# Linear attention and a swish MLP on one core: batch 0 by halves of its heads, and the order of two sets of sums in block 6

## The chip, the cores and the metric

The kernel runs on one core of one Trainium2 chip. The metric is device time in microseconds (us). Engines are named as in the profile: PE (TensorE matmul), PEld (its weight loads), DVE (VectorE), ACT (ScalarE), POOL (GpSimd) and SP (SyncE, which only issues transfers here).

## The reference

Linear attention over 8 batches of 8 heads, 576 tokens and 64 features a head, then an MLP from 512 to 2048 and back over all 4608 tokens. Inputs and output are float32; the kernel works in bf16 with float32 sums.

```python
def phi(x):
    return np.where(x > 0, x, np.exp(x) - 1.0) + 1.0
q_p, k_p = (phi(q), phi(k))
kv = np.einsum('bhsd,bhse->bhde', k_p, v)
z = np.sum(k_p, axis=2)
num = np.einsum('bhsd,bhde->bhse', q_p, kv)
den = np.einsum('bhsd,bhd->bhs', q_p, z)[..., None] + 1e-06
x = (num / den).transpose(0, 2, 1, 3).reshape(B * S, H * D)
h = x @ w_in
g = h * (1.0 / (1.0 + np.exp(-beta * h)))
y = g @ w_out
```

## The kernel before

The order of the instructions on every engine is written out by hand. Work goes in blocks: block b computes h, g and y of batch b, and the attention of the batches after it (phi, kv, numerators) is put between the products as side work. Of a batch's 576 tokens, 512 go through its block as four tiles of 128; the ninth part of all batches (64 tokens each, `xT_tail`) makes a ninth block of 512 at the end. h is made in 16 tiles of 128 features ("f tiles"); each goes through silu on ACT into `g_sb`.

**Start.** Batch 0 has nothing to hide behind, so its attention is PE's critical work. SP loads q and k of batch 0 in two halves each (heads 0 to 3 and 4 to 7, called `pr` 0 and 1). POOL issues, in this order, v of batch 0 in two halves, w_in in four parts, two parts of w_out, q and k of batch 1 (`load`, L99); the last two wait for v's halves, whose counters they take over. phi is exp on ACT (`phi_exp`), max on DVE (`phi_relu`) and min on DVE (`phi_min`). PE transposes phi of q (`q_half`, `q_last` for the last 64 tokens) into banks from which `q_copy` and `q_copy_last` fill `qT`.

Then, for all heads at once: `z_sums` (L519) sums phi of k over the tokens, half by half; `kv_first` (L530) makes k'v; `zbd` (L557) and `kv_mask` (L539) put both into block form on DVE; `denom_mm` (L571) makes the denominators of a token tile for all heads, `denom` (L578) adds 1e-6 and inverts. `numer_first` (L591) makes a token tile's numerators for all heads and multiplies on DVE into `xs_sb` (L595, 512 columns); `x_first` transposes the tile's four 128x128 parts on PE (L385) and copies them into `xT` (L242 on ACT). `h_first(t)` adds the products of the four k parts for token tile t in f tiles 0 to 3, 16 products of 128 columns (L405). The last, half token tile (t = 4) goes to `xT_tail` before `h_first(3)`. After that f tiles 4 to 15 run plain, with four products of 512 columns each, and then Y of batch 0 (L420).

`idle(n)` is n products of 512 columns on constant data, which keep PE at work.

PSUM has two pools of four banks in this stage: `bank` (tag h) and `bank1` (tag f). Tiles take the banks in turn, so a tile waits for the last reader of the tile four before it. `hp0`, the four h banks of f tiles 0 to 3, come from the first pool behind the denominators; f tiles 4 to 7 from the second, behind the numerators and transposes.

**Y of a block** (`y_fast`, L1003) computes the 512x512 output by seven products of 16 instructions in four banks pa, pd, pc and pb, with DVE's sums between:

```python
product(pc, sums(1), wsum(1), True, step=4 if b == 1 else 8)
nc.vector.tensor_add(u2, pc, r1)
nc.vector.tensor_add(u3, pd, u2)
run(side, 3)
```

(L1025 to L1028; `run(side, n)` runs the side work of place n there.) Behind it follow pb, a second product into pd (L1038) and one into pb. Before each block from 3 on, `h_x_sums` (L822) makes four sums of the next block's x, which read `xT` after its transposes (SP, L358). Blocks 7 and 8 use more sums of w_in: `h_w_sums(2)` (L800 to L803) runs in Y of block 6. In Y of block 6 the x sums stand at place 0, ahead of u2 and u3 (L1026, L1027), and the w_in sums at place 4.

Of the kernel before, what the change touches and what calls it, by code (L numbers as in the profile page):

```python
# [16 lines left out]
def kernel(  # L17
# [33 lines left out]
    def bank(name, shape=None, dt=F32):  # L51
        return hps.tile(shape or [P, 512], dt, tag="h", name=name)

    def bank1(name, shape=None, dt=F32):
        return fps.tile(shape or [P, 512], dt, tag="f", name=name)
# [89 lines left out]
    for i in range(2):  # L145
        nc.vector.memset(vaug[i][:, :, :, :, D : D + 2], 1.0)

    warm_ps = bank("warm_ps")

    def idle(n, ps=None):  # L150
# [119 lines left out]
    def q_tile(b):  # L270
        st[b, "qT"] = work.tile([P, 2, NT, 2, P], BF16, tag="qT", name="qT", bufs=1)
# [16 lines left out]
    def rows_of(t):  # L288
        return P if t < NT - 1 else G
# [106 lines left out]
            )  # L396


    def h_mm(x, ff, hp, c0=0, c1=512, kcs=range(KC)):
        for kc in kcs:  # L400
            if x is xT_tail:
                n, xm = G, x[:, kc % 2, :, kc // 2]
            else:
                n, xm = P, x[:, kc % 2, 2 * (c0 // P) + kc // 2 : 2 * (c1 // P) : 2]
            nc.tensor.matmul(  # L405
                hp[:, c0:c1].rearrange("p (t n) -> p t n", n=n),
                w_in_sb[ff // 4][:, kc, (ff % 4) * P : (ff % 4 + 1) * P],
                xm,
                start=(kc == 0), stop=(kc == KC - 1), skip_group_check=True,
            )  # L410

    def silu(b, ff, hp):
# [79 lines left out]
    phi_tile(0, "q")  # L492
    phi_tile(0, "k")
    q_tile(0)
    qtp = [bank1("qtp", [P, 1024], BF16) for _ in range(2)]
    phi_part(0, "q", 0)
    q_half(0, 0, qtp[0])
    idle(4)
    phi_part(0, "q", 1)
    q_half(0, 1, qtp[1])  # L500
    t8 = bank1("qtp8", [P, 2 * P], BF16)
    q_last(0, t8)
    bps = bank("bps", [P, FC])
    nc.tensor.matmul(bps, beta_row, ident16, is_transpose=True, start=True, stop=True)
    idle(4)
    x = xin(0, "k", 0)
    phi_exp(0, "k", 0, x)
    phi_relu(0, "k", 0, x)
    q_copy(nc.vector, 0, 0, qtp[0])
    phi_min(0, "k", 0)  # L510


    zps = [bank("zps") for _ in range(2)]
    zbd = consts.tile([P, 2, 2, 2], BF16)

    def z_sums(pr):
        for j in range(J):
# [3 lines left out]
                    start=(j == 0), stop=(j == J - 1), skip_group_check=True,  # L521
                )

    kvp0 = [[bank1("kvp0") for _ in range(2)] for _ in range(2)]
    kv0 = consts.tile([P, 2, 2, 2 * D], BF16)

    def kv_first(pr):
        for j in range(J):
# [8 lines left out]
    def kv_mask(pr):  # L537
        for hh in range(2):
            nc.vector.tensor_mul(  # L539
                kv0[:, hh, pr].rearrange("p (h d) -> p h d", h=2),  # L540
                kvp0[pr][hh][:, 0:P].rearrange("p (h d) -> p h d", h=2),
                kvmask[:, hh, :, 0:D],
            )

    z_sums(0)
    idle(3)
    phi_part(0, "k", 1)
    q_copy(nc.scalar, 0, 1, qtp[1])
    q_copy_last(nc.scalar, 0, t8)
    nc.scalar.copy(beta_s, bps)  # L550
    table(ACTF.Silu)
    kv_first(0)
    z_sums(1)
    idle(1)
    kv_first(1)
    for hh in range(2):
        nc.vector.tensor_mul(  # L557
            zbd[:, hh], zps[hh][:, 0:2, None].to_broadcast([P, 2, 2]), kvmask[:, :, :, 0]
        )
    kv_mask(0)  # L560

    dps = [bank("dps", [P, NT, 8]) for _ in range(2)]
    den0 = [consts.tile([P, NT, 8], F32, name=f"den0{i}") for i in range(2)]
    rden0 = [consts.tile([P, NT, 8], F32, name=f"rden0{i}") for i in range(2)]

    def denom_mm(t):
        n = rows_of(t)
        for hh in range(2):
            for pr in range(2):
                c = 4 * hh + 2 * pr  # L570
                nc.tensor.matmul(  # L571
                    dps[t > 1][:n, t, c : c + 2], st[0, "qT"][:, pr, t, hh, 0:n],
                    zbd[:, hh, pr, :], start=True, stop=True, skip_group_check=True,
                )

    def denom(r, t0, t1):
        i, ts = t0 > 1, slice(t0, t1)
        nc.vector.tensor_scalar(den0[i][:r, ts], dps[i][:r, ts], 1e-6, None, ALU.add)  # L578
        nc.vector.reciprocal(rden0[i][:r, ts], den0[i][:r, ts])

    for t in range(NT):
        denom_mm(t)
    kv_mask(1)
    denom(P, 0, 2)

    def numer_first(t):
        n = rows_of(t)
        nps = bank1("nps0", [P, 2, 2, P])
        for hh in range(2):
            for pr in range(2):  # L590
                nc.tensor.matmul(  # L591
                    nps[:n, hh, pr], st[0, "qT"][:, pr, t, hh, 0:n], kv0[:, hh, pr, :],
                    start=True, stop=True, skip_group_check=True,
                )
        nc.vector.tensor_mul(  # L595
            xs_tile(0, t),
            nps[:n].rearrange("p a b (c d) -> p a (b c) d", d=D),
            rden0[t > 1][:n, t].rearrange("p (a i) -> p a i", a=2)[:, :, :, None].to_broadcast(
                [n, 2, 4, D]
            ),  # L600
        )

    def x_first(t, eng):
        x_trans(0, t, eng, bank1("xtp0", [P, KC, P], BF16))


    hp0 = []

    def h_first(t):
        if len(hp0) < 4:  # L610
            hp0.extend(bank("h_ps") for _ in range(2))
        for ff in range(4):
            h_mm(xT[0], ff, hp0[ff], t * P, (t + 1) * P)


    hp0.extend(bank("h_ps") for _ in range(2))
    for t in range(3):
        numer_first(t)
        if t == 1:
            denom(P, 2, NT - 1)  # L620
    idle(2, hp0[0])
    denom(G, NT - 1, NT)
    x_first(0, nc.scalar)
    numer_first(3)
    x_first(1, nc.scalar)
    h_first(0)
    numer_first(4)
    x_first(2, nc.scalar)
    h_first(1)
    x_first(3, nc.scalar)  # L630
    nc.vector.tensor_mul(beta_m, beta_s, beta_s)
    nc.vector.tensor_scalar(beta_m, beta_m, TINY * TINY, 2.0 * TINY, ALU.is_lt, ALU.mult)
    nc.vector.tensor_add(beta_c, beta_s, beta_m)
    nc.vector.reciprocal(rbeta, beta_c)
    h_first(2)
    x_first(4, nc.vector)
    h_first(3)
    for ff in range(4):
        silu(0, ff, hp0[ff])
    for ff in range(4, 8):  # L640
        hp = bank1("h_ps")
        h_mm(xT[0], ff, hp)
        silu(0, ff, hp)
    first.close()
    wps = ctx.enter_context(tc.tile_pool(name="wps", bufs=2, space=bass.MemoryType.PSUM))
    load_w_out(2)
# [427 lines left out]
    for b in range(1, B + 1):  # L1074
        n, m = b + 1, b + 2
        sh, sy = {}, {}
        if b == 2 or b == B - 1:
            at(sh, 0, lambda: tail_copy(b))
        if n < B:
            at(sh, 0, lambda: next_loads(n))  # L1080
            if b > 2:
                at(sh, 0, lambda: tail_copy(b))
            at(sh, {1: 9, 2: 3}.get(b, 0), lambda: kv_both(n))
            at(sh, {1: 11, 2: 5}.get(b, 10), lambda: numer_all(n))
        if b == 1:
            at(sh, 4, lambda: w_sum(2))
            at(sh, 9, lambda: w_sum(1))
            at(sy, 0, lambda: w_sum(3))
        if m < B:
            at(sy, 0, lambda: phi_tile(m, "q"), lambda: phi_tile(m, "k"))  # L1090
            if b == 1:

                for pr in range(2):
                    at(sy, 0, lambda pr=pr: phi_exp(m, "q", pr, xin(m, "q", pr)))
                    at(sy, 2, lambda pr=pr: phi_relu(m, "q", pr, xin(m, "q", pr)))
                    at(sy, 3 + pr, lambda pr=pr: phi_min(m, "q", pr))
                for pr in range(2):
                    at(sy, 0, lambda pr=pr: v_copy(nc.scalar, m, pr))
                at(sy, 4, lambda: q_trans_dma(m))
                for pr in range(2):  # L1100
                    at(sy, 5, lambda pr=pr: phi_exp(m, "k", pr, xin(m, "k", pr)))
                    at(sy, 5, lambda pr=pr: phi_relu(m, "k", pr, xin(m, "k", pr)))
                    at(sy, 6, lambda pr=pr: phi_min(m, "k", pr))
                at(sy, 6, lambda: table(ACTF.Silu))
            else:
                at(sy, 0, lambda: phi_part(m, "q", 0))
                at(sy, 1, lambda: phi_part(m, "q", 1))
                at(sy, 1, lambda: q_trans_dma(m))
                at(sy, 4, lambda: phi_part(m, "k", 0))
                at(sy, 4, lambda: phi_part(m, "k", 1), lambda: table(ACTF.Silu))  # L1110
        if b == 2:
            at(sh, 2, lambda: h_w_sums(0))
        if b == B - 2:
            at(sy, 4, lambda: h_w_sums(2))
        if 2 <= b < B:
            at(sy, 6 if b < B - 2 else 0, lambda: h_x_sums(n))
        (h_phase if b < 3 else h_fast)(b, xT[b % 2] if b < B else xT_tail, sh)
        y_fast(b, sy)

# [29 lines left out]
```

## Time and profile before

| what | value |
|---|---|
| three runs | 273.04, 273.45, 274.24 us, median 273.45 |
| profiled execution | 273.47 us, its span 271.7 us |
| mean granted TensorE clock | 0.999 |
| busy share of PE, DVE, ACT, POOL | 97%, 76%, 62%, 16% |
| first h product of batch 0 | 16.77 us |
| Y of batch 0 begins | 32.17 us |
| idle of PE before yd in Y of block 6 | 1.40 us |

Times within the span count from its start. A row of a timeline gives start, duration, engine, line, operation, out<-in, shape and count, and in brackets the engine's idle time before it with what ended it. A row of the chain gives start, duration, engine and tile. The DVE and PE timelines show the end of one instruction after the start of the next, since they are pipelined: 16 products of 256 columns follow each other at 1.75 us and are listed with 1.91.

### The profile page before, as it was taken

The page shows a single profiled execution, that of the slowest core. Times are in us where ns is not written, and L with a number is a line of the kernel's source. Part 1 is how long each engine was busy: PE and PEld are TensorE (multiplying, and loading weights), DVE is VectorE, ACT ScalarE, POOL GpSimd, SP SyncE. Part 2 cuts the span into 40 slices and gives each one's busy share as a digit, 9 for nine tenths or more (in the row PEclk, how much of TensorE's full clock was granted, in tenths as well). Part 3 has the DMA queues.
Part 4 walks back from the last instruction along what each step waited for, and adds up shares of the span by engine and source line. Part 5 has one row for each costly group of instructions (what it writes and reads, how often), then busy time and mean ns, then how long its engine had stood idle before and what let it go on. Part 6 is the DMA issues. An engine that isn't in the chain of part 4 may idle for free.

```text
span 271.7 us, 6793 instructions
## 1 busy us (share of the span) xinstructions
PE 263.0 (97%) x2859; PEld 181.3 (67%) x2865; DVE 207.1 (76%) x404; ACT 167.4 (62%) x236; POOL 43.6 (16%) x65
## 2 busy tenths in 40 slices
PE   7799999999999999999999999999999799999994
PEld 3485455446865587658765876588658666886793
DVE  4871786999996579689968986899686877856862
ACT  5738894977965893599349934994492038405810
POOL 5922005040105003030213003310000100000000
PEclk9999999999999999999999999999999999999999
DMA  7999999997599945995699559945504050023013
GB/s 252 240 207 351 249 320 249 273 183 258 90 247 191 187 78 99 281 210 72 109 257 232 85 91 273 232 86 96 148 7 85 0 154 4 0 51 106 0 41 116
DMA packets 49214, 42.19 MB, mean 155 GB/s; under 512 B 30352, under 2 KB 41248, under 8 KB 49184
## 3 DMA queue, kind: packets, MB, share of 16 engines
q0 software_dynamic: 13296, 22.81, 37.3%
q1 hardware_dynamic: 35568, 18.75, 31.0%
q8 instruction: 22, 0.36, 0.5%
q10 hardware_dynamic: 320, 0.20, 0.2%
q14 instruction: 8, 0.07, 0.1%
HBM read 36.71 MB, written 9.44 MB: 170 GB/s over the span
## 4 chain that ended last, share of the span: by engine, by line
PE 89%; DMA 4%; DVE 2%; SPq 2%; issue 1%; ACT 0%; DVEq 0%; ACTq 0%
PE h_ps L405 36%; PE yd L1003 10%; PE ya L1003 9%; PE yb L1003 8%; PE hc L837 5%; PE yc L1003 5%; PE y_ps L420 4%; PE hz L837 4%; DMA stage<-in_k_dram 3%; PE kvp L226 2%; PE nps L336 2%; DMA xT<-xs_sb 2%; PE yb L975 1%; SPq L358 1%; PE xtp L385 1%
## 5 line engine op out<-in xcount | busy, mean ns | idle before, releaser
L413 ACT ACTIVATE g<-h_ps,beta_c 128x512 bf16<-128x512 f32 x112 | 74.6, 690 | 63.0 <-PE h_ps L405 62.5
L405 PE MATMUL h_ps<-xT,w_in 128*128 128x512 bf16 (+1 forms) x464 | 97.6, 357 | 0.1
L405 PEld LDWEIGHTS <-w_in 128*128 128x128 bf16 x496 | 44.8, 98 | 40.7 <-issue 0.2
L1003 PEld LDWEIGHTS <-stage 128*128 128x128 bf16 x480 | 47.0, 98 | 5.5
L1003 PEld LDWEIGHTS <-g 128*128 128x128 bf16 x384 | 37.5, 98 | 7.6 <-issue 1.6
L1003 PE MATMUL ya<-w_out,g 128*128 128x256 bf16 x256 | 30.6, 273 | 0.0
L351 DVE TENSOR_TENSOR xs_sb<-nps,rden 128x448 bf16<-128x448 f32 (+2 forms) x24 | 18.2, 758 | 0.8
L164 ACT ACTIVATE e<-xk 128x1152 bf16<-128x1152 bf16 (+1 forms) x15 | 16.7, 1159 | 0.2 <-DMA xk<-in_k_dram 0.2
L1003 PE MATMUL yd<-ws,g 128*128 128x256 bf16 x128 | 15.3, 273 | 1.4 <-DVE u L1027 1.4
L164 ACT ACTIVATE e<-xq 128x1152 bf16<-128x1152 bf16 x14 | 15.6, 1160 | 0.0
L157 ACT ACT_TABLE_LOAD x12 | 15.4, 1283 | 0.2
L1003 PE MATMUL yc<-ws,stage 128*128 128x256 bf16 x128 | 15.3, 273 | 0.0
L1003 PE MATMUL yd<-ws,stage 128*128 128x256 bf16 x128 | 15.3, 273 | 0.0
L244 POOL CAST vaug<-vf 128x1152 bf16<-128x1152 f32 x10 | 11.4, 1175 | 22.1 <-DMA vf<-in_v_dram 22.1
L420 PE MATMUL y_ps<-w_out,g 128*128 128x512 bf16 x60 | 14.4, 379 | 0.3 <-issue 0.2
L887 ACT ACTIVATE g<-hc,beta_c 128x512 bf16<-128x512 f32 x16 | 10.1, 683 | 6.4 <-DVE hc L873 6.4
L177 DVE TENSOR_TENSOR phi_q<-e,r 128x1152 bf16<-128x1152 bf16 x16 | 12.1, 757 | 2.3 <-ACT e L164 1.3
L177 DVE TENSOR_TENSOR phi_k<-e,r 128x1152 bf16<-128x1152 bf16 x16 | 12.7, 802 | 1.5 <-DVE r L171 0.5
L746 DVE TENSOR_TENSOR stage<-g 128x1024 bf16<-128x1024 bf16 x16 | 11.0, 686 | 3.2 <-ACT g L413 3.2
L1003 PE MATMUL yb<-w_out,stage 128*128 128x256 bf16 x112 | 13.4, 272 | 0.0
L1003 PE MATMUL yb<-ws,stage 128*128 128x256 bf16 x112 | 13.4, 273 | 0.0
L837 PEld LDWEIGHTS <-w_in 128*128 128x128 bf16 x96 | 9.4, 98 | 4.5
(139 smaller groups left out, 359.2 us busy)
## 6 DMA issues: line engine op xcount, KB each, us to landing
out_dram<-y SPq DMA_DIRECT2D x29, 256.0 KB, 3.8
vf<-in_v_dram POOLq DMA_DIRECT2D x6, 1152.0 KB, 9.1
xq<-in_q_dram POOLq DMA_DIRECT2D x7, 576.0 KB, 12.4
xk<-in_k_dram POOLq DMA_DIRECT2D x7, 576.0 KB, 14.5
w_in<-in_moe_w_in_dram POOLq DMA_DIRECT2D x4, 512.0 KB, 11.7
g<-in_moe_w_out_dram POOLq DMA_DIRECT2D x2, 1024.0 KB, 17.2
stage<-in_moe_w_out_dram POOLq DMA_DIRECT2D x2, 1024.0 KB, 20.9
stage<-in_q_dram SPq DMA_DIRECT2D x2, 576.0 KB, 4.2
```

Source lines behind the costliest of these rows:

```text
L157: nc.scalar.activation(act0, warm[:, 0:1], func)
L164: nc.scalar.activation(e, x, ACTF.Exp)
L177: nc.vector.tensor_tensor(st[b, a][:, pr].rearrange("p j (h d) -> p j h d", h=2), st[b, a, pr, "e"].rearrange("p h j d -> p j h d"), st[b, ...
L244: eng.tensor_copy(dst, src)
L351: nc.vector.tensor_mul(xs_sb[:, ils, v0 * D : v1 * D].rearrange("p i (u d) -> p i u d", d=D), pv[:, :, :, 0:D], rden[:, :, :, None].to_bro ...
L405: nc.tensor.matmul(hp[:, c0:c1].rearrange("p (t n) -> p t n", n=n), w_in_sb[ff // 4][:, kc, (ff % 4) * P : (ff % 4 + 1) * P], xm, start=(k ...
L413: nc.scalar.activation(g_sb[b % 2][:, ff, :], hp, ACTF.Silu, scale=beta_c[:, ff : ff + 1])
L420: nc.tensor.matmul(yp[:, c0:c1], g_sb[b % 2][:, ff, t * P : (t + 1) * P], w_out_sb[i][:, c, c0:c1], start=(ff == 0), stop=(ff == FC - 1), ...
L746: nc.vector.tensor_add(gs[0][:, c], g[:, c, HM:512], g[:, c2, HM:512])
L837: nc.tensor.matmul(o, lhs[:, i, a * P : (a + 1) * P], m, start=(first and a == 0 and i == 0), stop=True, skip_group_check=True,)
L887: nc.scalar.activation(g_sb[b % 2][:, ff].rearrange("p (t n) -> p t n", t=2), src, ACTF.Silu, scale=beta_c[:, ff : ff + 1],)
L1003: nc.tensor.matmul(ps[:, p * HM : (p + 1) * HM], lhs(c, p), rhs(c), start=(first and p == 0 and c == 0), stop=True, skip_group_check=True,)
```

## The change

Batch 0's attention goes by halves of the heads. `z_mask(pr)`, `denom_mm(pr)`, `denom(pr)`, `numer_first(pr, t, o)`, `x_first(pr, ...)` and `trans_first(pr, ...)` work on four heads; two token tiles share a bank and, but for tiles 0 and 1 of the first half, one DVE multiplication and one ACT copy. `h_first(pr, t0, n)` adds that half's two k parts, for one or two token tiles. `denom_mm` runs all token tiles in full width, so the unused columns of `qT`'s tile 4 are set to zero by a memset on POOL. The first `q_copy` goes from DVE to ACT. The half token tile's numerators and transposes move behind f tiles 4 and 5. Three `idle` products are dropped. In Y of block 6 the w_in sums move from place 4 to place 0, and the x sums from place 0 to place 4.

```diff
+    nc.gpsimd.memset(st[0, "qT"][:, :, NT - 1, :, G:P], 0.0)
     qtp = [bank1("qtp", [P, 1024], BF16) for _ in range(2)]
     phi_part(0, "q", 0)
     q_half(0, 0, qtp[0])
     idle(4)
     phi_part(0, "q", 1)
+    q_copy(nc.scalar, 0, 0, qtp[0])
     q_half(0, 1, qtp[1])
...
-    q_copy(nc.vector, 0, 0, qtp[0])
...
+    def denom_mm(pr):
+        dps.append(bank("dps", [P, NT, 2, 2]))
+        for t in range(NT):
+            for hh in range(2):
                 nc.tensor.matmul(
+                    dps[pr][:, t, :, hh], st[0, "qT"][:, pr, t, hh, :], zbd[pr][:, hh],
...
+    def h_first(pr, t0, n=1):
...
+            h_mm(
+                xT[0], ff, hp0[ff], t0 * P, (t0 + n) * P, kcs=(2 * pr, 2 * pr + 1),
+                first=(t0 == 0),
+            )
+
+    z_sums(0)
+    idle(2)
+    x = xin(0, "k", 1)
+    phi_exp(0, "k", 1, x)
+    phi_relu(0, "k", 1, x)
+    z_mask(0)
+    phi_min(0, "k", 1)
+    q_copy_last(nc.scalar, 0, t8)
+    nc.scalar.copy(beta_s, bps)
+    q_copy(nc.scalar, 0, 1, qtp[1])
+    table(ACTF.Silu)
+    denom_mm(0)
+    denom(0)
+    kv_first(0)
+    kv_mask(0)
+    z_sums(1)
+    idle(1)
+    z_mask(1)
+    kv_first(1)
+    kv_mask(1)
+    nps0 = [numer_two(0, g) for g in range(2)]
+    x_first(0, nps0[0], 0)
+    tp = tp_bank()
+    trans_first(0, tp, 0)
+    denom_mm(1)
+    nps1 = [numer_two(1, 0)]
     hp0.extend(bank("h_ps") for _ in range(2))
...
+    x_first(0, nps0[0], 1)
+    x_first(0, nps0[1], 2, 2)
+    denom(1)
+    h_first(0, 0)
+    trans_first(0, tp, 1)
+    nps1.append(numer_two(1, 1))
+    tp = tp_bank()
+    trans_first(0, tp, 2, 2)
+    x_first(1, nps1[0], 0, 2)
+    h_first(0, 1)
+    tp = tp_bank()
+    trans_first(1, tp, 0, 2)
+    x_first(1, nps1[1], 2, 2)
+    h_first(0, 2, 2)
+    tp = tp_bank()
+    trans_first(1, tp, 2, 2)
...
+    h_first(1, 0, 2)
+    h_first(1, 2, 2)
     for ff in range(4):
         silu(0, ff, hp0[ff])
...
+    h_plain(4)
+    nps4 = bank1("nps0", [P, 2, 256])
+    for pr in range(2):
+        numer_first(pr, NT - 1, nps4[:G, pr])
...
+    h_plain(5)
+    x_trans(0, NT - 1, nc.vector, tp_bank())
+    h_plain(6)
+    h_plain(7)
...
         if b == B - 2:
-            at(sy, 4, lambda: h_w_sums(2))
+            at(sy, 0, lambda: h_w_sums(2))
         if 2 <= b < B:
-            at(sy, 6 if b < B - 2 else 0, lambda: h_x_sums(n))
+            at(sy, {B - 2: 4, B - 1: 0}.get(b, 6), lambda: h_x_sums(n))
```

More of the change, by code (lines that the diff above doesn't have):

```diff
@@ L146 @@
         nc.vector.memset(vaug[i][:, :, :, :, D : D + 2], 1.0)
+    bps = bank("bps", [P, FC])
     warm_ps = bank("warm_ps")
@@ L396, in x_trans_dma, with h_mm @@
             )
-    def h_mm(x, ff, hp, c0=0, c1=512, kcs=range(KC)):
+    def h_mm(x, ff, hp, c0=0, c1=512, kcs=range(KC), first=True):
         for kc in kcs:
@@ L408, in h_mm @@
                 xm,
-                start=(kc == 0), stop=(kc == KC - 1), skip_group_check=True,
+                start=(first and kc == 0), stop=(kc == KC - 1), skip_group_check=True,
             )
@@ L502 @@
     q_last(0, t8)
-    bps = bank("bps", [P, FC])
     nc.tensor.matmul(bps, beta_row, ident16, is_transpose=True, start=True, stop=True)
     idle(4)
-    x = xin(0, "k", 0)
-    phi_exp(0, "k", 0, x)
-    phi_relu(0, "k", 0, x)
-    q_copy(nc.vector, 0, 0, qtp[0])
-    phi_min(0, "k", 0)
-    zps = [bank("zps") for _ in range(2)]
-    zbd = consts.tile([P, 2, 2, 2], BF16)
+    phi_part(0, "k", 0)
+    zps = [bank("zps") for _ in range(2)]
+    zbd = [consts.tile([P, 2, 2], BF16, name=f"zbd{i}") for i in range(2)]
+    kvp0 = [[bank1("kvp0") for _ in range(2)] for _ in range(2)]
+    kv0 = [consts.tile([P, 2, 2 * D], BF16, name=f"kv0{i}") for i in range(2)]
+    den0 = consts.tile([P, 2, NT, 4], F32)
+    rden0 = consts.tile([P, 2, NT, 4], F32)
+    dps = []
+    xs0 = xs_sb.rearrange("p i n -> p (i n)")
     def z_sums(pr):
@@ L522, in z_sums, with z_mask @@
                 )
-    kvp0 = [[bank1("kvp0") for _ in range(2)] for _ in range(2)]
-    kv0 = consts.tile([P, 2, 2, 2 * D], BF16)
+    def z_mask(pr):
+        for hh in range(2):
+            nc.vector.tensor_mul(
+                zbd[pr][:, hh], zps[hh][:, pr : pr + 1].to_broadcast([P, 2]),
+                kvmask[:, pr, :, 0],
+            )
     def kv_first(pr):
@@ L539, in kv_mask @@
             nc.vector.tensor_mul(
-                kv0[:, hh, pr].rearrange("p (h d) -> p h d", h=2),
+                kv0[pr][:, hh].rearrange("p (h d) -> p h d", h=2),
                 kvp0[pr][hh][:, 0:P].rearrange("p (h d) -> p h d", h=2),
@@ L543, in kv_mask @@
             )
[L545 to L570, printed above, removed]
-                nc.tensor.matmul(
[L572 to L592, printed above, removed]
+    def denom_mm(pr):
+        dps.append(bank("dps", [P, NT, 2, 2]))
+        for t in range(NT):
+            for hh in range(2):
+                nc.tensor.matmul(
+                    dps[pr][:, t, :, hh], st[0, "qT"][:, pr, t, hh, :], zbd[pr][:, hh],
@@ L593, in numer_first, with denom @@
                     start=True, stop=True, skip_group_check=True,
                 )
-        nc.vector.tensor_mul(
[L596 to L600, printed above, removed]
-        )
-    def x_first(t, eng):
-        x_trans(0, t, eng, bank1("xtp0", [P, KC, P], BF16))
+    def denom(pr):
+        dv = dps[pr].rearrange("p t i a -> p t (i a)")
+        nc.vector.tensor_scalar(den0[:, pr], dv, 1e-6, None, ALU.add)
+        nc.vector.reciprocal(rden0[:, pr], den0[:, pr])
@@ new lines, in numer_first, with numer_two, x_first @@
+    def numer_first(pr, t, o):
+        for hh in range(2):
+            nc.tensor.matmul(
+                o.rearrange("p (i a d) -> p a i d", i=2, a=2)[:, hh],
+                st[0, "qT"][:, pr, t, hh, 0 : rows_of(t)], kv0[pr][:, hh],
+                start=True, stop=True, skip_group_check=True,
+            )
+    def numer_two(pr, g):
+        nps = bank1("nps0", [P, 2, 256])
+        for n in range(2):
+            numer_first(pr, 2 * g + n, nps[:, n])
+        return nps
+    def x_first(pr, nps, t0, n=1):
+        nc.vector.tensor_mul(
+            xs0[:, t0 * DM : (t0 + n) * DM].rearrange(
+                "p (t r c d) -> p t r c d", r=2, c=4, d=D
+            )[:, :, pr],
+            nps[:, t0 % 2 : t0 % 2 + n].rearrange("p t (c d) -> p t c d", d=D),
+            rden0[:, pr, t0 : t0 + n, :, None].to_broadcast([P, n, 4, D]),
+        )
@@ new lines, in trans_first @@
+    def trans_first(pr, tp, t0, n=1):
+        c = slice(2 * (t0 % 2), 2 * (t0 % 2 + n))
+        for k in range(2 * n):
+            x0 = (t0 + k // 2) * DM + (2 * pr + k % 2) * P
+            nc.tensor.matmul(
+                tp[:, c][:, k], xs0[:, x0 : x0 + P], identity,
+                is_transpose=True, start=True, stop=True, skip_group_check=True,
+            )
+        nc.scalar.copy(
+            xT[0][:, :, 2 * t0 + pr : 2 * (t0 + n) : 2].rearrange("p i t n -> p t i n"),
+            tp[:, c].rearrange("p (t i) n -> p t i n", i=2),
+        )
@@ L607, with tp_bank @@
+    def tp_bank():
+        return bank1("xtp0", [P, KC, P], BF16)
     hp0 = []
-    def h_first(t):
+    def h_first(pr, t0, n=1):
         if len(hp0) < 4:
@@ L612, in h_first @@
         for ff in range(4):
-            h_mm(xT[0], ff, hp0[ff], t * P, (t + 1) * P)
-    hp0.extend(bank("h_ps") for _ in range(2))
[L617 to L630, printed above, removed]
+            h_mm(
+                xT[0], ff, hp0[ff], t0 * P, (t0 + n) * P, kcs=(2 * pr, 2 * pr + 1),
+                first=(t0 == 0),
+            )
+    z_sums(0)
[24 more added lines that the diff above has]
+    nps1 = [numer_two(1, 0)]
+    hp0.extend(bank("h_ps") for _ in range(2))
+    x_first(0, nps0[0], 1)
[14 more added lines that the diff above has]
+    trans_first(1, tp, 2, 2)
     nc.vector.tensor_mul(beta_m, beta_s, beta_s)
@@ L634, with h_plain @@
     nc.vector.reciprocal(rbeta, beta_c)
-    h_first(2)
-    x_first(4, nc.vector)
-    h_first(3)
+    h_first(1, 0, 2)
+    h_first(1, 2, 2)
     for ff in range(4):
         silu(0, ff, hp0[ff])
-    for ff in range(4, 8):
+    def h_plain(ff):
         hp = bank1("h_ps")
@@ L643 @@
         silu(0, ff, hp)
+    h_plain(4)
+    nps4 = bank1("nps0", [P, 2, 256])
+    for pr in range(2):
+        numer_first(pr, NT - 1, nps4[:G, pr])
+    xs_tile(0, NT - 1)
+    nc.vector.tensor_mul(
+        xs0[:G, (NT - 1) * DM : NT * DM].rearrange("p (r c d) -> p r c d", r=2, d=D),
+        nps4[:G].rearrange("p r (c d) -> p r c d", d=D),
+        rden0[:G, :, NT - 1, :, None].to_broadcast([G, 2, 4, D]),
+    )
+    h_plain(5)
+    x_trans(0, NT - 1, nc.vector, tp_bank())
+    h_plain(6)
+    h_plain(7)
     first.close()
```

## The prediction

> **What bounds the kernel now.** The profiled execution took 273.47 us: a span of 271.7 and 1.77 around it. The three timed runs have their median at 273.45 (273.04 to 274.24), so sums are made against 273.47. I read the page first: busy time by engine, then the chain that ended last.
>
> ```profile
> PE 263.0 (97%) x2859; PEld 181.3 (67%) x2865; DVE 207.1 (76%) x404; ACT 167.4 (62%) x236; POOL 43.6 (16%) x65
> ...
> PE 89%; DMA 4%; DVE 2%; SPq 2%; issue 1%; ACT 0%; DVEq 0%; ACTq 0%
> ```
>
> TensorE is the bound, and time moves only where PE stands still or does more. The change touches two such places. The chain in order of time, first 52 us:
>
> ```profile
> 12.14 0.61 PE kvp L530 x18
> ...
> 16.77 1.13 PE h_ps L405 x16
> ...
> 20.81 11.36 PE h_ps L405 x64
> 32.17 1.08 PE y_ps L420 x5
> ```
>
> The first h products start at 16.77. The 64 in the third row are h_first(3) (16, 0.89) and the twelve plain f tiles, so f tile 4 starts at 21.70 and Y of batch 0 at 32.17. From 32.17 to 41.3 PE does not wait, so what the start-up loses is passed on whole.
>
> The timeline of POOL, start and duration:
>
> ```profile
> 0.73 0.20 POOL masks.py:197 MEMSET identity<- 128x128 bf16 x1 [0.29 <-POOLq L1133]
> ...
> 1.56 0.52 POOL L119 MEMSET kv_bd<- 128x520 bf16 x1
> ...
> 11.92 0.77 POOL L99 DMA_DIRECT2D xq<-in_q_dram  x1
> 13.14 0.75 POOL L99 DMA_DIRECT2D xk<-in_k_dram  x1 [0.45 <-DMA vf<-in_v_dram]
> ```
>
> The last row matters most: POOL stands in front of xk's load until v's second half has landed, and is free again at 13.89.
>
> The timeline of DVE where start-up meets the loads:
>
> ```profile
> 34.50 0.83 DVE L171 TENSOR_SCALAR r<-xk 128x1152 bf16<-128x1152 bf16 x2 [0.86 <-DMA xk<-in_k_dram]
> ...
> 37.13 1.67 DVE L456 TENSOR_SCALAR w_out<-stage,rbeta 128x512 bf16<-128x512 f32 x4
> ...
> 40.05 1.41 DVE L244 COPY vaug<-vf 128x1152 bf16<-128x1152 bf16 x2
> ```
>
> The stage tile's answer gives that w_out load 21.0 us from its issue at 16.10 to landing, so it landed at 37.1; the DVE work up to the vaug copies, which end at 41.46, cannot start earlier.
>
> Block 6, the timelines of DVE and of PE:
>
> ```profile
> 207.38 0.69 DVE L748 TENSOR_TENSOR stage<-g,stage 128x1024 bf16<-128x1024 bf16 x1
> 210.74 0.43 DVE L822 TENSOR_TENSOR xs_sb<-xT 128x512 bf16<-128x512 bf16 x1 [2.67 <-DMA xT<-xs_sb]
> ...
> 212.29 0.68 DVE L1026 TENSOR_TENSOR u<-yc,r 128x512 f32<-128x512 f32 x1
> 213.01 0.69 DVE L1027 TENSOR_TENSOR u<-yd,u 128x512 f32<-128x512 f32 x1
> ```
>
> ```profile
> 210.44 1.91 PE L1003 MATMUL yb<-ws,stage 128*128 128x256 bf16 x16
> 213.75 1.91 PE L1003 MATMUL yd<-ws,g 128*128 128x256 bf16 x16 [1.40 <-DVE u L1027]
> ```
>
> DVE waits 2.67 us for the transposes with u2 (L1026) and u3 (L1027) queued behind; PE waits for u3, since its next product goes into the bank that u3 reads.
>
> **Block 6: minus 1.56 us.** The four w_in sums (0.41 to 0.43 each, 1.54 from 214.40 to 215.94) move into the idle 2.67: 208.07 to 209.6. They need no transpose. yc is complete at about 210.6 (208.69 plus 1.91), so u2 runs then and u3 ends near 212.03. yd would follow yb at the 1.75 step of all these products: 210.44 + 1.75 = 212.19 instead of 213.75. What is late next is u3 itself, by a margin of 0.1; block 5 has the same (u3 ends 184.62, yd starts 184.75 without a wait). The x sums (four, 1.57) now stand behind the addition to y2, from about 213.05 to 214.6; the transposes landed by 210.7. Behind them wait the y2 addition of pd (214.5 to 215.2, whose bank the next block's first plain tile needs at 216.1) and hz, which needs the second x sum at 215.7. Both have 0.9 or more. SP's stores go out no later than before. Between 1.2 (some of u3's margin gone) and 1.65.
>
> **Start-up: plus 1.7 us.** The instruction counts hardly change: 20 denominators, 20 numerators, 20 transposes, and the same 8192 columns of h in 40 products for 64; three warm-up products fewer. What changes is order, and one new wait.
>
> Before the wait there is a gain. qT's first copy goes from DVE (0.67) to ACT, where 1.02 (the 128x1024 row at 39.65) fits between the exp that ends at 7.08 and k's landing at 8.6. phi_k starts at 9.86 instead of 10.21, the z sums end at 11.05, the z mask at 11.55. denom_mm(0) takes the bank of beta's transpose, so it waits for ACT: exp to 11.19, last q copy 0.38 (the 64x260 row), beta 0.19, hence 11.7. Its tiles 0 to 3 are through at 12.0.
>
> Tile 4 now reads qT in full width, so its weight load waits for the new memset. In the changed program that memset stands on POOL right behind xk's load: it starts at 13.89, takes 0.31 (between 0.20 for 128 columns and 0.52 for 520), and PE goes on at about 14.29. PE stands still for 2.3 us, and kv_first(0), z_sums(1), kv_first(1) and all numerators are queued behind; on DVE, denom(0) waits with both kv masks behind it. On POOL only w_out's next load stands behind the memset, and that waits until 16.10 anyway (idle 2.21 before it).
>
> From there by the rows: denominators 0.07, kv_first 0.56, z sums 0.32, one warm-up 0.29, kv_first 0.61: 16.14, complete 16.21. kv_mask(1) 16.24 to 16.72. The first x tile (256 columns; 0.62 for 448 and 0.69 for 512 give 0.42) ends at 17.06; two transposes and 0.33 to ACT (half of four's 0.44 and a fixed part), a 256-column copy 0.38, and the first h product starts at 17.86 instead of 16.77: plus 1.09. From then PE has 4.68 without a real gap: h 0.45, 0.45 and three of 0.88, transposes 0.78, numerators 0.26, one wait of 0.1, so f tile 4 starts at 22.54 instead of 21.70: plus 0.84. Tile 4's numerators (0.34) and transposes (0.22) have moved behind it: plus 0.56. Last, f tile 6 takes f tile 4's bank, with numerators and transposes using the two banks between. The first silu can start at about 22.05; silus follow each other at 0.59, so the fifth ends at 25.1 where PE comes at 24.8: plus 0.33. Sum 1.73, unknowns from 1.1 (no bank wait, memset at 0.2) to 2.4 (memset at 0.52, each hop 0.1 longer). The changed order on DVE (masks twice, denominators per half) costs nothing of itself: PE is the late one from 17.9 on.
>
> Nothing later gives this back: silu, exp and so phi and vaug shift with PE, and the loads are early for a later PE.
>
> Sum: 273.47 - 1.56 + 1.73 = 273.6 us.
>
> **Rivals.** (a) The memset does not hold PE (POOL is through with xk early, or v lands earlier). For it: without that wait the same walk starts 2.25 earlier, Y of batch 0 starts at 31.6 instead of 32.17. Against: the 0.45 row and the order on POOL. Even so little is kept: the vaug copies end at 41.46 because of the landing at 37.1, and PE needs the second one 0.39 after 41.30, a slack of 0.23. Time 273.47 - 1.56 - 0.23 = 271.7. It decides if the memset ends before 12.0.
>
> (b) Slower: the stall lets the TensorE clock fall. Price: the 14 warm-up products at 1.46 took 4.91, where 0.216 each would be 3.0, so a cold start costs 1.9; here the dense stretch from 15 on would pay it: 273.6 + 1.9 = 275.5. It decides if 2.3 us of standing still are enough. Against: the windows answer has a granted clock of 1.00 in 10 to 12 us with PE busy 0.95 of 2, and 1.00 through the 1.40 us wait of block 6. [...]
>
> (c) Slower: block 6 keeps its wait, because u3 is late for another reason (the margin is only 0.1, and if the x sums' transposes or the w_in sums reach past 210.6, u2 waits again). Then the 1.56 is not gained: 275.1. Against: the sums need 1.54 of 2.67 idle us.
>
> **The numbers.** About 0.5% (1.37 us) is what a measurement of this kernel can tell from no change. Forecast 0.66, its own range 272.9 to 274.7 (-1.65 + 1.1 and -1.2 + 2.4); (a) 0.14; (b) 0.12; (c) 0.08. The forecast lies within 0.5%: same 0.66; (a) faster 0.14; (b) and (c) slower 0.20. The range takes in the forecast's own range and (a): 271.6 to 274.7.
>
> **What would show it.** POOL: a memset of qT at 13.9. PE: an idle of some 2.3 us ended by POOL at the denominators (L571 before), first h product near 17.9, f tile 4 near 22.5, Y of batch 0 near 33.9. ACT's fifth silu ends as f tile 6 starts. Block 6: DVE's w_in sums between 208 and 210 plus the shift, and no idle on PE before yd. I am wrong if PE waits at the denominators for less than 1 us, if the granted clock drops below 1 around 15 us, if Y of batch 0 starts before 32.9, or if yd still waits for u3.

## The result, and the profile after

| kernel | median, us | lowest to highest, us | runs |
|---|---|---|---|
| before | 273.30 | 273.04 to 274.24 | 22 |
| after | 274.27 | 273.26 to 275.81 | 22 |

The ratio is 1.0033 (95%: 1.002 to 1.0046): a third of a per cent slower, inside the forecast's range and inside the 0.5% that count as no change. Sorted by the mean granted clock the 22 runs of after are three groups: 6 runs of 273.26 to 273.45 at 1.00, 13 of 274.22 to 274.51 at 0.991 to 0.994, and 3 of 275.37 to 275.81 at 0.986. The profiled execution (274.40, span 272.6, clock 0.994) is one of the middle group.

The page of after, busy time and the shares of the chain that ended last:

```profile
PE 263.1 (97%) x2833; PEld 181.6 (67%) x2838; DVE 206.6 (76%) x404; ACT 168.5 (62%) x238; POOL 43.3 (16%) x66
...
PE 93%; POOL 3%; DMA 1%; DVE 1%; issue 0%
```

TensorE is still the bound, with 27 weight loads fewer than before (2838 for 2865). The memset and the stall, in the timelines of POOL and then of PE:

```profile
12.76 0.78 POOL L99 DMA_DIRECT2D xk<-in_k_dram  x1
13.50 0.37 POOL L497 MEMSET qT<- 128x256 bf16 x1
```

```profile
13.92 0.20 PE L559 MATMUL dps<-zbd,qT 128*128 128x2 bf16 x2 [2.38 <-POOL qT L497]
14.06 0.85 PE L539 MATMUL kvp<-vf,phi_k 64*128 64x128 bf16 x18
```

The memset stands on POOL where the forecast put it, and PE waits 2.38 us for it. Then comes what the forecast gave a chance of 0.12. The answer by stretches (stretch, length, busy us and instructions of PE, PEld, DVE, ACT, POOL, then granted clock, DMA share, GB/s):

```profile
12.00:14.00 2.00, 0.08 (x2) 0.08 (x2) 0.00 (x0) 1.33 (x2) 1.87 (x4) 1.00 1.24 207
14.00:16.00 2.00, 2.00 (x47) 1.53 (x49) 1.08 (x6) 0.00 (x0) 0.45 (x1) 0.60 1.24 207
16.00:18.00 2.00, 1.91 (x27) 1.45 (x24) 1.17 (x5) 0.00 (x0) 0.38 (x2) 0.54 1.26 213
18.00:20.00 2.00, 1.99 (x39) 1.76 (x37) 1.86 (x6) 0.99 (x3) 0.67 (x1) 1.00 1.23 201
```

PE works 0.08 of the 2 us from 12 to 14, and the clock falls to half behind it: in the trace from 14.41 to 17.83, 3.41 us, which the stretches show as 0.60 and 0.54. The chain in order of time shows what the half clock stretches:

```profile
13.54 0.33 POOL qT L497
13.92 0.20 PE dps L559 x2
...
15.67 1.08 PE kvp L539 x18
...
18.57 0.59 PE h_ps L406 x8
...
25.80 8.74 PE h_ps L406 x40
34.54 1.08 PE y_ps L421 x5
```

The second kv_first takes 1.08 (0.61 in the chain of before), the first h product starts at 18.57, Y of batch 0 at 34.54 instead of 32.17: 2.37 late. Block 6, the timelines of DVE and PE:

```profile
211.59 0.62 DVE L851 TENSOR_TENSOR vf<-w_in,vf 128x512 bf16<-128x512 bf16 x1
213.18 0.69 DVE L1074 TENSOR_TENSOR u<-yc,r 128x512 f32<-128x512 f32 x1 [0.98 <-PE yc L1051]
213.91 0.69 DVE L1075 TENSOR_TENSOR u<-yd,u 128x512 f32<-128x512 f32 x1
215.47 0.41 DVE L870 TENSOR_TENSOR xs_sb<-xT 128x512 bf16<-128x512 bf16 x1
```

```profile
212.91 1.91 PE L1051 MATMUL yb<-ws,stage 128*128 128x256 bf16 x16
214.66 1.91 PE L1051 MATMUL yd<-ws,g 128*128 128x256 bf16 x16
```

yd follows yb at 1.75 and no bracket stands behind it: the 1.40 us wait is gone. From the first product of Y (ya) to yd it is 8.73 here (205.93 to 214.66) and 10.30 before (203.45 to 213.75): minus 1.57. The two together are 2.37 - 1.57 = 0.8, against 0.9 between the spans.

### The profile page after: what moved, and what is told of

Its sections match the earlier page's. It is cut to its first block, busy times and chain, and to the rows that moved or that the text cites. A ratio compares the mean times of both kernels' runs of the same rounds, so it can differ in the third digit from the quotient of the medians.

```text
span 272.6 us, 6745 instructions
## 1 busy us (share of the span) xinstructions
PE 263.1 (97%) x2833; PEld 181.6 (67%) x2838; DVE 206.6 (76%) x404; ACT 168.5 (62%) x238; POOL 43.3 (16%) x66
## 4 chain that ended last, share of the span: by engine, by line
PE 93%; POOL 3%; DMA 1%; DVE 1%; issue 0%
PE h_ps L406 36%; PE yd L1051 10%; PE ya L1051 10%; PE yb L1051 9%; PE hc L885 5%; PE yc L1051 5%; PE y_ps L421 5%; PE hz L885 4%; PE kvp L227 2%; PE nps L337 2%; DMA stage<-in_q_dram 1%; PE yb L1023 1%; POOL w_in L129 1%; PE kvp L539 1%; POOL g L132 1%; POOL vf L99 1%
## 5 line engine op out<-in xcount | busy, mean ns | idle before, releaser
L406 PE MATMUL h_ps<-xT,w_in 128*128 128x512 bf16 (+2 forms) x440 | 97.8, 368 | 0.0
```

The lines of the kernel that those rows point to most:

```text
L406: nc.tensor.matmul(hp[:, c0:c1].rearrange("p (t n) -> p t n", n=n), w_in_sb[ff // 4][:, kc, (ff % 4) * P : (ff % 4 + 1) * P], xm, start=(f ...
```

## The experiments

In each table the first column is what ran. The median of before on the same chip was 273.30 in the first set (e1 to e4) and 273.34 in the second (e5 to e8).

### e1: no wait for the memset

After, with qT's memset right behind kv_bd's, where it starts at 2.03:

```diff
     nc.gpsimd.memset(kv_bd, 0.0)
+    qT0 = work.tile([P, 2, NT, 2, P], BF16, tag="qT", name="qT", bufs=1)
+    nc.gpsimd.memset(qT0[:, :, NT - 1, :, G:P], 0.0)
...
+    st[0, "qT"] = qT0
...
-    q_tile(0)
-
-    nc.gpsimd.memset(st[0, "qT"][:, :, NT - 1, :, G:P], 0.0)
```

> The whole change, but qT's memset stands on POOL right behind kv_bd's, at about 2 us, where POOL is idle. If the wait of tile 4's weight load is what the start-up loses by, PE has no idle of 2 us at the denominators, the granted clock stays 1.00, Y of batch 0 starts near 31.6 us, and the time is 271.5 to 271.8 (block 6 gives 1.56, the start-up only 0.2 because vaug waits for w_out's landing at 37.1). Rival 1, the halving itself costs the start-up (more hops between PE, DVE and ACT): Y of batch 0 stays behind 32.5 and the time near 273.3. Rival 2, there is no cap behind the start: all of the 0.6 is kept and the time is 271.1.

| | median, us | range | runs | ratio (95%) | clock |
|---|---|---|---|---|---|
| e1 | 271.67 | 271.54 to 271.87 | 5 | 0.9938 (0.9927 to 0.995) | 0.997 to 1.00 |

As expected in its time. In PE's timeline Y of batch 0 starts at 30.91, where before has 32.00: 1.1 earlier. Then the cap shows. Timeline of PE, then of DVE:

```profile
40.73 0.48 PE L230 MATMUL kvp<-vaug,phi_k 64*64 64x65 bf16 x36 [0.45 <-DVE vaug L248]
41.38 0.48 PE L230 MATMUL kvp<-vaug,phi_k 64*64 64x65 bf16 x36 [0.18 <-DVE vaug L248]
```

```profile
37.00 1.67 DVE L460 TENSOR_SCALAR w_out<-stage,rbeta 128x512 bf16<-128x512 f32 x4 [0.46 <-DMA stage<-in_moe_w_out_dram]
...
39.93 1.40 DVE L248 COPY vaug<-vf 128x1152 bf16<-128x1152 bf16 x2
```

PE now waits for both vaug copies, and those stand behind a scaling that waits for w_out's landing at 37.0, as before.

### e2: the exchange of the sums alone

Before, with these lines of the change and nothing else:

```diff
-            at(sy, 4, lambda: h_w_sums(2))
+            at(sy, 0, lambda: h_w_sums(2))
...
-            at(sy, 6 if b < B - 2 else 0, lambda: h_x_sums(n))
+            at(sy, {B - 2: 4, B - 1: 0}.get(b, 6), lambda: h_x_sums(n))
```

> The kernel before with only the two sets of sums in block 6 exchanged. Theory: minus 1.56, so 271.7 to 271.9, no idle on PE before the second product into pd, and all else as before. Rival: another wait takes its place (u3, the x sums or hz) and the time stays above 272.8.

| | median, us | range | runs | ratio (95%) |
|---|---|---|---|---|
| e2 | 271.63 | 271.60 to 271.72 | 5 | 0.9937 (0.9925 to 0.9948) |

It gains 1.67, as much as e1, which has the start-up by halves besides. So the start-up by halves, freed of its wait, adds nothing here: most of the 1.1 that e1 gains up to Y of batch 0 is lost again, 0.63 of it in the two waits for the vaug copies. The first ya of block 1 starts at 65.68 in e1 and at 65.64 in e2.

### e3: the start-up alone

After, with the old order of the sums (e2's lines the other way round).

> The start-up by halves with the wait on the memset, block 6 as before. Theory: plus 1.6 where the clock does not fall (274.9) and a further 1.0 where it does (275.8); with the second run above, the two parts add up to the whole change. Rival: the parts do not add (some of the start-up's loss comes back in block 6): under 274.3.

| | median, us | range | runs | ratio (95%) |
|---|---|---|---|---|
| e3 | 274.46 | 273.33 to 275.47 | 10 | 1.0045 (1.003 to 1.006) |

A miss: the rival is right that the parts do not add. By the forecast's working this kernel should lack the gain of 1.56 in block 6, but its runs fall into the groups of after: one at 273.33 with a clock of 1.00, six at 274.20 to 274.74, three at 275.23 to 275.47. Its start is as late as after's (Y of batch 0 at 34.45), and yet the wait of block 6 is gone, though the x sums stand in front of u2 as before. Timelines of DVE and PE:

```profile
211.29 0.42 DVE L870 TENSOR_TENSOR xs_sb<-xT 128x512 bf16<-128x512 bf16 x1 [0.96 <-DMA xT<-xs_sb]
```

```profile
212.70 1.91 PE L1051 MATMUL yb<-ws,stage 128*128 128x256 bf16 x16
214.45 1.91 PE L1051 MATMUL yd<-ws,g 128*128 128x256 bf16 x16
```

DVE waits 0.96 for the transposes instead of 2.67: the last of them took 2.63 from issue to landing, where before it took 4.34. In the trace of before 15 of its 16 arrivals come by 208.88, the last at 210.62. What lies there is a packet of another queue; the answer on the DMA of before from 208.4 to 208.7:

```profile
q8 instruction: 1, 0.02, 18.2%
q1 hardware_dynamic: 7, 0.00, 2.6%
```

Queue q8, of the kind "instruction", has 22 packets of 16 KB in the span. This one starts at 208.56 and takes 0.88, just as the last transpose's packets come in. In all ten traces the packet at this place comes behind 4764 to 4780 records of PE (products and weight loads), though their starts differ by up to 54 of them; so these packets are taken to be PE's instructions, and their place to be set by how many PE has executed. That is inferred from the counts, not shown by the trace itself. The start-up by halves has 27 products and 27 weight loads fewer (24 of h, 3 for warmth), so the packet comes later in block 6. e6 below tests this.

### e4: PE kept at work in the stall

After, with nine products on constant data ahead of tile 4's denominators:

```diff
         for t in range(NT):
+            if pr == 0 and t == NT - 1:
+                idle(9)
```

> The whole change, with nine warm-up products of 512 columns on constant data ahead of tile 4's denominators, so that PE works (1.94 us) while it would stand still. They end before the memset does and delay nothing. Theory: the wait on POOL stays, but the granted clock is 1.00 in all runs and the time is 273.3 in every one, instead of 273.3 in some and 274.3 in most. Rival: the fall of the clock does not come from PE's idle time (it is the chip's, or comes from the transfers): the times stay spread, with a median of 274.3.

| | median, us | range | runs | ratio (95%) | clock |
|---|---|---|---|---|---|
| e4 | 273.38 | 273.28 to 273.98 | 12 | 1.0002 (0.9994 to 1.0011) | 0.997 to 1.00 |

As expected: the clock falls in none of the 12 runs, and the median is 0.9 below after's. By stretches:

```profile
12.00:14.00 2.00, 2.00 (x16) 0.80 (x12) 0.43 (x1) 1.97 (x3) 1.31 (x2) 1.00 1.23 204
14.00:16.00 2.00, 1.64 (x50) 1.25 (x51) 1.08 (x6) 0.20 (x1) 0.42 (x2) 1.00 1.24 206
```

The memset still holds the denominators (in the profiled run until 14.48, since v's second half landed late), but PE is at work and the clock column stays at 1.00. So the runs of after that take longer are those in which the clock falls, and with PE at work in the stall it falls in 0 of 12 runs instead of 16 of 22.

### e5 and e6: the place of the instruction packet

Both are e3 (old order of the sums) with the stall filled: e5 with `idle(9)`, which leaves PE 18 products short of before; e6 with 27 products, so that PE's count up to block 6 is that of before again (the edit as against e5):

```diff
             if pr == 0 and t == NT - 1:
-                idle(9)
+                idle(7)
+                tiny(20)
...
+    def tiny(n):
+        for _ in range(n):
+            nc.tensor.matmul(
+                warm_ps[:, 0:1], warm[:, 0:P], warm[:, 0:1], start=True, stop=True
+            )
```

> The start-up by halves with nine warm-up products in the stall (so that the clock does not fall), block 6 as before. The run of the start-up alone, where Y of batch 0 began 2.3 us late and the time was yet only 0 to 0.9 above before, asks where the rest came back. Theory: PE's wait in Y of block 6 comes from a 16 KB fetch of instructions (queue q8) that runs on one of the 16 DMA engines from 208.56 to 209.4 and holds the last of the 16 arrivals of x's last transpose (15 were there by 208.9, the last at 210.6). PE fetches at a fixed number of its instructions; the start-up by halves has 53 fewer, so the fetch comes some 2.3 us later against block 6 and meets no transpose. With 18 instructions added back it still comes after them: time 273.3 to 273.5, no idle before yd. Rival: the wait is paid, and the start-up by halves is worth 1.5 without a fallen clock: 274.9.

> As the run before it, but with seven warm-up products of 512 columns and twenty of one column in the stall: 27 pairs, so that PE has as many instructions ahead of block 6 as the kernel before. Nothing else differs; both fill less than the stall. Theory: the fetch falls on the last transpose again, PE waits 1.4 before yd, time 274.8 to 275.0. Rival: the wait has to do with when block 6 runs, or with other transfers, and not with PE's number of instructions: 273.4, no wait.

| | median, us | range | runs | ratio (95%) |
|---|---|---|---|---|
| e5 | 273.44 | 273.27 to 274.46 | 10 | 1.0002 (0.9993 to 1.0011) |
| e6 | 274.88 | 274.77 to 275.11 | 4 | 1.0056 (1.0043 to 1.0069) |

Both as expected: 18 idle products of no use, some 200 us earlier, cost 1.44 us between the medians. (e5's profiled run is its slowest, 274.46: v's second half landed late there and PE went on at 15.07. Its block 6 has no idle before yd all the same.) In e6 the wait is back. Timeline of DVE, then of PE, then the chain:

```profile
212.15 0.42 DVE L879 TENSOR_TENSOR xs_sb<-xT 128x512 bf16<-128x512 bf16 x1 [2.55 <-DMA xT<-xs_sb]
```

```profile
215.16 1.91 PE L1060 MATMUL yd<-ws,g 128*128 128x256 bf16 x16 [1.28 <-DVE u L1084]
```

```profile
207.80 4.23 DMA xT<-xs_sb
215.16 1.91 PE yd L1060 x16
```

The packet's place in every kernel, from the traces (weight loads of PE as the profile's page counts them; the packet's start is measured from the first ya of block 6; e7 and e8 follow below):

| kernel | PEld | ya starts | packet starts | behind ya | last transpose, issue to landing |
|---|---|---|---|---|---|
| before | 2865 | 203.45 | 208.56 | 5.11 | 4.34 |
| e2 | 2865 | 203.15 | 208.27 | 5.12 | 4.31 |
| e6 | 2865 | 204.98 | 209.97 | 4.99 | 4.23 |
| e5 | 2847 | 206.00 | 212.65 | 6.65 | 2.62 |
| e4 | 2847 | 205.51 | 212.16 | 6.65 | 2.62 |
| after | 2838 | 205.93 | 213.31 | 7.38 | 2.64 |
| e3 | 2838 | 205.71 | 213.14 | 7.43 | 2.63 |
| e1 | 2838 | 203.22 | 210.57 | 7.35 | 2.63 |
| e7 | 2838 | 203.32 | 210.73 | 7.41 | 2.62 |
| e8 | 2838 | 203.68 | 211.64 | 7.96 | 2.62 |

The fewer instructions PE has had, the later the packet, whatever the start or the order of the sums (e8 lies 0.5 behind the other four with its count, for a reason not looked for); and the last transpose is late in just those three kernels where the packet lies 5 us behind ya. e2 has the late landing too and does not pay: its x sums stand behind u2 and u3. That is the exchange doing what it says, on a wait that the other part of the change has already moved away.

The same pair of events stands elsewhere in the traces. Of 364 DMA transposes in the ten traces, ten have their last arrival 1.55 to 1.73 us behind the fifteenth; in all others it is 0.56 at most. In each of the ten a packet of q8 starts 0.32 to 0.64 us ahead of the fifteenth arrival, and of the other 354 only three have one there. Three of the ten are those of block 6; behind the other seven PE does not wait, so they cost nothing. The packet goes with the late arrival; by what path it would delay it, no trace shows.

### e7: e1 with the old order of the sums

> qT's memset early, and the sums of block 6 in the order of before. Theory: 53 fewer instructions alone move the fetch away, so the time is 271.7 without the exchange, as with it (271.67), and yd does not wait. Rival: the exchange is what removes the wait: 273.2.

| | median, us | range | runs | ratio (95%) |
|---|---|---|---|---|
| e7 | 271.78 | 271.75 to 271.84 | 4 | 0.9942 (0.9929 to 0.9955) |

As expected, and within 0.11 of e1. In its trace yb starts at 210.31 and yd at 212.06, without a wait: with the packet elsewhere the exchange is worth nothing that these runs can tell.

### e8: the cap, with half the scaling on POOL

e1, and of the four scalings behind w_out's last landing two on POOL:

```diff
-    w_out_scale(nc.vector, 2)
+    w_out_scale(nc.vector, 2, range(2))
+    w_out_scale(nc.gpsimd, 2, range(2, 4))
```

> The whole change with the memset early, and two of the four scalings of w_out's third part on POOL instead of DVE. In the run with the early memset Y of batch 0 began at 31.06, 1.1 earlier than before, and PE then waited 0.45 and 0.18 for the vaug copies, which end at 41.3 because DVE waits for w_out's landing at 37.0 and has 4.5 of work behind it. Theory: DVE saves 0.8 there, but v's landing at 39.7 and 1.4 of copies hold the end of vaug at 41.1, so only 0.2 comes out: 271.4 to 271.55. Rival 1: the 0.8 is kept as far as PE can use it: 271.1. Rival 2: POOL's scalings (0.69 each) disturb DVE or come too late for Y: 271.7 or more.

| | median, us | range | runs | ratio (95%) |
|---|---|---|---|---|
| e8 | 271.94 | 271.85 to 273.10 | 6 | 0.9955 (0.994 to 0.997) |

A miss: no gain over e1, and rival 2 holds (271.7 or more). Timelines of POOL and of DVE:

```profile
37.42 2.32 POOL L460 TENSOR_SCALAR w_out<-stage,rbeta 128x512 bf16<-128x512 f32 x2 [9.66 <-DMA stage<-in_moe_w_out_dram]
```

```profile
37.27 1.33 DVE L460 TENSOR_SCALAR w_out<-stage,rbeta 128x512 bf16<-128x512 f32 x2 [0.47 <-DMA stage<-in_moe_w_out_dram]
38.52 1.82 DVE L181 TENSOR_TENSOR phi_k<-e,r 128x1152 bf16<-128x1152 bf16 x2
40.26 1.40 DVE L248 COPY vaug<-vf 128x1152 bf16<-128x1152 bf16 x2
```

Side by side the scalings take longer. By the trace's single instructions, DVE's first takes 0.49, as it does alone, and its second 0.93; POOL's two take 0.90 and 1.42, where 0.69 is usual; of the two phi_k behind, the second takes 1.16 instead of 0.75. The vaug copies end at 41.7, where e1's end at 41.3. The landing was 0.27 later here, and from it to the end of the copies it is 4.4 us in e8 and 4.3 in e1: the work taken off DVE saved nothing. What makes them longer side by side, the trace does not show.

## Why the prediction was right, and where its steps were not

**The time.** Forecast 273.6; the six runs of after without a fall of the clock lie at 273.3, the median of all 22 at 274.27. So the forecast's own sum holds for the undisturbed clock. Sixteen of the 22 runs had rival (b) besides, and that the median of all 22 still lies in the range is luck: its upper end of 274.7 was made of a longer start-up and a smaller gain in block 6, not of the clock.

**Start-up, plus 1.73.** e4's profiled run shows the walk at full clock. There PE goes on at 14.48, 0.19 later than forecast (14.29), the first h product starts at 18.10 (17.86 + 0.19 = 18.05) and Y of batch 0 at 34.07 (33.9 + 0.19 = 34.09). Inside it two terms are off and cancel, by luck: f tile 4 starts at 22.93 (22.54 + 0.19 = 22.73), 0.2 late, and the bank wait of f tile 6, put at 0.33, is 0.01. The first silu starts 0.61 ahead of f tile 4 instead of 0.49, so the fifth ends at 25.32 as PE comes at 25.33. In after the memset took 0.37 instead of 0.31, but v landed earlier, so POOL did not stand at all in front of xk's load and PE went on at 13.92 instead of 14.29. The row that the forecast says matters most, POOL's wait for v, was therefore not what held the memset there. POOL's own DMA issues were: in the chain of after ten of them follow each other from 5.59 to 13.54, about 0.8 each, and the memset stands behind the last.

**Block 6, minus 1.56.** The number is right (1.57, and 1.67 in e2), u3's margin too (it ends at 214.60, yd starts at 214.66). The step that failed is one that was not worked out: that block 6 only shifts with the start-up and its wait belongs to the order of the sums alone. The wait needed a landing 1.7 us late as well, and the late landing goes with an instruction packet whose place the start-up moves (e5 and e6). So the two terms are not two independent terms: without the exchange the sum is the same (e3, e5), and without the start-up the exchange gains all of it (e2). The forecast counted the 24 h products and three warm-up products that go, and looked only at their columns, not at their number.

**What is left over.** By the after profile a run without the fall has about 1.36 of start-up loss (1.73 less the 0.37 at the memset) and 1.57 of gain, which makes 273.1; the runs lie at 273.3 to 273.4. In the after profile 0.1 of this arises between Y of batch 0 (2.37 late) and the first ya of block 6 (2.48 late); the rest of these 0.2 to 0.3 was not traced.

**Rival (a).** The wait held PE, so it did not happen; its time of 271.7 was met by e1 (271.67), and its cap is the row with the 0.45 and 0.18 of waits. Only the 0.23 to be kept was too much: e1 is no faster than e2.

**Rival (b).** The step that failed is its chance. The forecast set 2.3 us of standing still against the 1.40 of block 6, through which the clock had stayed at 1.00. The clock fell in 16 of 22 runs and in 9 of 10 of e3. Its price was about 0.95 in 13 runs (274.22 to 274.51 against 273.26 to 273.45) and 2.0 to 2.5 in three, for a forecast of 1.9: that was the price of a whole cold start (the first 14 products of before in 4.91 us instead of 3.0), and here one stretch of 3.41 at half clock lies over a path that is partly DVE's (from tile 4's denominators to the first h product it is 4.65 in after and 3.62 in e4). In the three runs the mean clock is 0.014 short of full, where the profiled run with its one stretch is 0.006 short; that there are two stretches in them is an estimate from these two figures, and no profile shows it.

**Rival (c).** Did not happen.

**The signs.** Of the four signs named beforehand, three (a stall over 1 us, Y of batch 0 after 32.9, no wait of yd for u3) came as forecast. The fourth, a clock of 1.00 around 15 us, did not, and the forecast had said that it would then be wrong: for 16 of the 22 runs it was.

## What to carry to other kernels

Before a term is taken from a wait, ask what made the last arrival late: if 15 of a transfer's 16 arrivals are in and one is 1.7 us behind, look for an instruction packet there. An edit that changes PE's instruction count ahead of it can then move the wait: here 27 products fewer took it away and 18 more brought it back. Test each part of a change alone and both together; here the parts gain 0 (start-up at full clock) and 1.67 (sums), and the whole, at full clock, 0. Where a new wait makes PE stand still (2.38 us in after's profile), fill it or move what it waits for: one memset issued 11 us earlier on the same queue (2.03 for 13.50) is worth 2.6 us (274.27 to 271.67). Of a stall, note PE's busy time around it beside the longest idle: in after that idle was 2.38 us, and PE had worked for 1.03 of the 3.41 us ahead of the fall of the clock.

## What the runs showed of the hardware

**The clock fell behind 3.41 us in which PE had worked for 1.03 us in after and 1.48 in e3.** The half clock of after lasts 3.41 us (14.41 to 17.83). In its trace the clock is full for 10.240 us ahead of the fall, at half for 3.413 and then full for 256.000, and in that of before it is full for 266.240: 3, 1, 75 and 78 times 3.413. The stretches of the table are 3.41 us long; those of after and before lie whole multiples of 3.413 from a change of the clock, that of e3 ends at its fall and that of e6 begins with its wait of 1.28 us before yd. PE's busy time in a stretch, and the clock behind it:

| kernel | stretch, us | PE busy, us | clock behind |
|---|---|---|---|
| after | 11.00 to 14.41 | 1.03 | half |
| e3 | 12.00 to 15.41 | 1.48 | half |
| after | 267.00 to 270.41 | 1.85 | full |
| e6 | 213.89 to 217.31 | 2.15 | full |
| before | 8.38 to 11.79 | 2.36 | full |

Of these five stretches 1.48 is the most that a fall stands behind and 1.85 the least that none stands behind. The longest idle of PE in the first is 2.38 us. The forecast's two cases against a fall were busy for more than the 1.48: of the 0.95 in the 2 us at 10 to 12 the most lies in the 2.36 of the last row, and the stretch with most of the 1.40 us wait of block 6 (209.76 to 213.18) has 2.59. That PE's busy time over such a stretch decides is the author's reading of these rows and was not tested by a run; how much of it is enough, and why 6 of 22 runs of after and 1 of 10 of e3 kept the clock, was not shown. The runs without a profile show neither their stretches nor their stall.

**In before a packet of an instruction queue goes with late data.** The profile's page of after has 22 packets, 0.36 MB on q8, 0.5% of the time of the 16 DMA engines. In before one of its packets of that queue, 0.88 us long, goes with one of a transpose's 16 arrivals coming 1.7 us late. Why it is twice the packet's own time was not settled, nor whether both used the same engine.
